# Filler matmuls in the opening of a convolution and gated feed-forward kernel: whole-array ones partly replaced by row halves and quarters

## The chip, the cores and the metric

The kernel runs on one core of one Trainium2 chip. The time is the device time of one execution in microseconds; the time before is 711.99 us, the median of three runs (711.8 to 712.13). The engines are named as in the profile: PE (TensorE matmuls) and PEld (its weight loads), DVE (VectorE), ACT (ScalarE), POOL (GpSimd) and SP (SyncE, which here only issues DMAs). PE multiplies a stationary operand (lhsT, loaded first) with a moving operand (rhs) and writes to PSUM.

## The reference

A causal convolution with a softmax over its seven taps, one tap set per head, and then a feed-forward layer whose activation is h * cos(h):

```python
w = softmax(weight)                        # 8 heads x 7 taps
x_pad = concat([zeros(6 rows), x], axis=1) # x: 8 x 4096 x 192
out[b, s, head, :] = sum_k w[head, k] * x_pad[b, s + k, head, :]   # 24 columns per head
h = out.reshape(32768, 192) @ w_in         # 192 x 2048
y = (h * cos(h)) @ w_out                   # 2048 x 192
```

Tensors come and go as float32; the kernel multiplies in bfloat16 and accumulates in float32.

## The kernel before

Tokens are handled in units of 1024 (32 units) and, for the feed-forward part, in tiles of 512 (64 tiles, t). The convolution of a unit is a matmul with a banded matrix `band` (128 x 256 per head, built from the softmax taps); its result is copied to `ct` in bfloat16, transposed to `cT` and used as the moving operand of the first feed-forward matmul.

For each tile t and each of eight j, `mm1` (L411) makes an h tile of 128 x 2 x 512: three pairs of matmuls, the two of a pair on rows 0 to 63 and 64 to 127 of the array, into the two PSUM banks of the tile. `gcu` takes the sine with a shift (ACT, L419) and multiplies it with h (DVE, L423) to give g. `mm2_step` (L458) multiplies g with w_out, again in pairs on the two row halves, 64 x 192 each, and accumulates in two banks `o_ps`. The h tiles come from a pool of three buffers, the h ring (`h_pool`); convolution results of later units use the ring as well. A new h tile can be written when the DVE product, or the copies, that read the old one are done.

The order of the work on PE and on ACT is written out by hand, in strings: `PE_FIRST[0]` for the first tile is "h0a h0b W0 h1 h2 h3 r h4 w5 d11 w4 h5 d21 W1 c11 X0 m1 h6 m11 h7 ...", where h is an mm1 (a and b its halves), m a number of mm2 steps, r, d and c convolution parts, w zero matmuls, W the cast of half of w_out, X the transpose through DMA. There is no reordering: each engine takes its queue in this order and waits where an operand or a buffer is not ready.

The opening, before that order starts, does the following. SP issues the load of the first half of unit 0 (`x_f`). DVE fills `zero`, 128 x 512 in bfloat16, with zeros. `keep_warm(n)` (L109) issues n matmuls of `zero` with `zero`, 128 x 128 stationary and 512 columns moving, into the bank `idle`; nobody reads the result. There are three of these, then the matmul that spreads the weights over the partitions (L123), then nine more. Meanwhile POOL, ACT and DVE make the softmax, a mask, `prod` and `diag` (L316, L319), and from `diag` the `band` in 16 small casts (L330, shared by DVE, POOL and ACT). ACT casts the first x to `x_bf` (L184).

`conv_first` (L347) is the next work in PE's queue after the nine: two halves of 16 matmuls with 48 columns, the first copied to `ct` by ACT, the second by DVE (L353). An SP instruction waits for the second copy and is followed on SP by four loads of w_out (`wo_f`, L97). `turn_first` (L368) transposes on PE and ACT and DVE copy the result to `cT` (L371); its four PSUM tiles are three from the h ring and one o bank. Then comes h0a, the first L411. POOL casts the x_f loads that follow (L184) and, behind them in its queue, the two halves of w_out (L93).

Of the kernel before, what the change touches and what calls it, by code (L numbers as in the profile page):

```python
# [8 lines left out]
FP32 = mybir.dt.float32  # L9
# [7 lines left out]
def kernel(  # L17
# [8 lines left out]
    nc = tc.nc  # L26
    B, S, D = x.shape
# [4 lines left out]
    T = 512  # L32
# [22 lines left out]
    h_pool = ctx.enter_context(tc.tile_pool(name="h_ps", bufs=3, space=PSUM))  # L55
# [47 lines left out]
    zero = consts.tile([128, T], BF16)  # L103
# [3 lines left out]
    def keep_warm(n, bank=idle):  # L107
        for _ in range(n):
            nc.tensor.matmul(out=bank, lhsT=zero[:, 0:128], rhs=zero, start=True, stop=True)  # L109
# [11 lines left out]
    w_all = o_pools[1].tile([128, T], FP32, name="o_ps1")  # L121
    w_bc = w_all[:, 0 : HQ * K].rearrange("p (h k) -> p h k", k=K)
    nc.tensor.matmul(out=w_all[:, 0 : HQ * K], lhsT=quarter, rhs=w_row, start=True, stop=True)  # L123
    keep_warm(9)


    xb0 = xbf_pool.tile([128, UB + 1, D], BF16, name="x_bf")
# [200 lines left out]
    for i, k in enumerate("DPDPDPDPDPDPDPAA"):  # L328
        q, rows = divmod(i, 4)
# [185 lines left out]
    for t in range(NT + 1):  # L515
# [6 lines left out]
        act, h = act.split(), {}  # L522
# [99 lines left out]
```

## Time and profile before

| | us |
|---|---|
| median of three runs | 711.99 (711.8 to 712.13) |
| the profiled execution, its own time | 711.61 |
| its span, first to last instruction | 709.9 |
| PE busy / DVE / ACT / POOL | 703.0 / 637.5 / 599.8 / 304.2 |
| first matmul | 1.31 |
| conv_first's first and last group start | 6.82, 7.90 |
| first L411 (h0a) | 10.62 |
| h7 of the first tile | 21.42 |

The page is of one profiled execution. Its times are relative to the first instruction of the program. "Busy" of PE counts the modelled length of each matmul, and matmuls overlap, so the distance from one start to the next tells the rate, and not the duration. A row of the timeline merges neighbouring instructions of one line: "x9" with a length of 3.13 are nine matmuls from the first start to the last end. A number in brackets is the idle time of that engine before the row, and the arrow names what ended it.

### The profile page before, as it was taken

The page shows a single profiled execution, that of the slowest core. Times are in us where ns is not written, and L with a number is a line of the kernel's source. Part 1 is how long each engine was busy: PE and PEld are TensorE (multiplying, and loading weights), DVE is VectorE, ACT ScalarE, POOL GpSimd, SP SyncE. Part 2 cuts the span into 40 slices and gives each one's busy share as a digit, 9 for nine tenths or more (in the row PEclk, how much of TensorE's full clock was granted, in tenths as well). Part 3 has the DMA queues.
Part 4 walks back from the last instruction along what each step waited for, and adds up shares of the span by engine and source line. Part 5 has one row for each costly group of instructions (what it writes and reads, how often), then busy time and mean ns, then how long its engine had stood idle before and what let it go on. Part 6 is the DMA issues. An engine that isn't in the chain of part 4 may idle for free.

```text
span 709.9 us, 26545 instructions
## 1 busy us (share of the span) xinstructions
PE 703.0 (99%) x11836; PEld 537.6 (76%) x11838; DVE 637.5 (90%) x598; ACT 599.8 (84%) x719; POOL 304.2 (43%) x308
## 2 busy tenths in 40 slices
PE   8999999999999999999999999999999999999997
PEld 4677777777777777777777777777777777777776
DVE  6889998998998999899999989989989999999996
ACT  7888888888888888888888888888888888888875
POOL 6653355333454433553434554335544335532400
PEclk9999999999999999999999999999999999999999
DMA  8954535535445455355354365553454554543411
GB/s 210 252 137 96 116 106 146 126 93 147 100 120 147 101 120 140 94 134 142 80 145 117 104 146 119 103 145 101 122 146 91 129 125 104 139 96 75 96 46 46
DMA packets 183713, 85.25 MB, mean 120 GB/s; under 512 B 111664, under 2 KB 183216, under 8 KB 183600
## 3 DMA queue, kind: packets, MB, share of 16 engines
q1 hardware_dynamic: 182888, 82.59, 47.9%
q8 instruction: 92, 1.51, 0.9%
q0 software_dynamic: 416, 0.79, 0.7%
q10 hardware_dynamic: 296, 0.20, 0.1%
q14 instruction: 21, 0.17, 0.1%
HBM read 31.36 MB, written 25.17 MB: 80 GB/s over the span
## 4 chain that ended last, share of the span: by engine, by line
PE 96%; DMA 1%; DVE 1%; POOL 0%; ACT 0%; SPq 0%; issue 0%; POOLq 0%
PE o_ps L458 47%; PE h L411 46%; PE h L196 3%; DMA x_f<-in_x_dram 1%; DVE g L423 0%; ACT cs L419 0%; PE h L458 0%; SPq L75 0%; POOL x_bf L184 0%; POOL mask L132 0%; PE o_ps L109 0%; ACT mask L137 0%; DVE diag L319 0%; DVE prod L316 0%; DVE o_sb L486 0%
## 5 line engine op out<-in xcount | busy, mean ns | idle before, releaser
L423 DVE TENSOR_TENSOR g<-h,cs 128x1024 bf16<-128x1024 f32 (+1 forms) x513 | 599.9, 1217 | 19.9 <-ACT cs L419 17.1
L419 ACT ACTIVATE cs<-h 128x1024 bf16<-128x1024 f32 (+1 forms) x513 | 514.4, 1022 | 85.1 <-PE h L411 64.9
L458 PEld LDWEIGHTS <-g 64*128 64x128 bf16 x8192 | 368.9, 94 | 91.6 <-DVE g L423 0.4
L458 PE MATMUL o_ps<-wo,g 64*128 64x192 bf16 x8128 | 434.8, 243 | 0.0
L411 PE MATMUL h<-cT,w 64*128 64x512 bf16 (+1 forms) x3078 | 412.2, 376 | 0.6 <-DVE g L423 0.3
L411 PEld LDWEIGHTS <-w 64*128 64x128 bf16 x3078 | 160.3, 94 | 67.4 <-issue 1.6
L302 POOL TENSOR_TENSOR edge_prod<-cT,tap 128x1008 f32<-128x1008 bf16 x30 | 67.2, 2241 | 281.7 <-DMA cT<-ct 281.7
L184 POOL CAST x_bf<-x_f 128x1728 bf16<-128x1728 f32 (+2 forms) x33 | 80.8, 2448 | 60.5 <-DMA x_f<-in_x_dram 42.3
L476 DVE COPY o_sb<-o_ps 128x384 f32<-128x384 f32 x62 | 34.6, 558 | 42.8 <-PE o_ps L458 42.6
L211 ACT CAST ct<-h 128x384 bf16<-128x384 f32 (+1 forms) x124 | 53.8, 484 | 14.0 <-PE h L196 13.4
L264 POOL COPY ct<-ct 128x1536 bf16<-128x1536 bf16 (+1 forms) x31 | 45.6, 1470 | 14.1 <-ACT ct L211 11.5
L196 PE MATMUL h<-x_bf,band 64*128 64x192 bf16 (+2 forms) x480 | 42.1, 243 | 0.1
L307 POOL TENSOR_TENSOR edge_prod<-edge_prod 128x144 f32<-128x144 f32 x60 | 33.3, 555 | 4.7
L305 POOL TENSOR_TENSOR edge_prod<-edge_prod 128x432 f32<-128x432 f32 x30 | 30.3, 1010 | 2.4
L476 ACT COPY o_sb<-o_ps 128x384 f32<-128x384 f32 x64 | 30.2, 474 | 0.1
L196 PEld LDWEIGHTS <-band 64*128 64x128 bf16 (+1 forms) x480 | 22.8, 94 | 1.5 <-issue 1.3
L308 POOL TENSOR_TENSOR cT<-edge_prod 128x144 bf16<-128x144 f32 x30 | 18.3, 610 | 2.4
L266 POOL COPY ct<-x_bf 128x192 bf16<-128x192 bf16 x60 | 19.2, 350 | 0.0
L109 PE MATMUL o_ps<-zero 128*128 128x512 bf16 x20 | 6.8, 476 | 1.4 <-DVE zero L104 1.3
L109 PEld LDWEIGHTS <-zero 128*128 128x128 bf16 x24 | 2.3, 110 | 4.2 <-issue 2.1
L93 POOL CAST wo<-wo_f 128x1536 bf16<-128x1536 f32 x2 | 2.9, 1469 | 2.4 <-DMA wo_f<-in_moe_w_out_dram 2.4
L458 PE MATMUL h<-wo,g 64*128 64x192 bf16 x64 | 3.2, 244 | 0.1
(61 smaller groups left out, 35.5 us busy)
## 6 DMA issues: line engine op xcount, KB each, us to landing
out_dram<-o_sb SPq DMA_DIRECT2D x63, 384.0 KB
x_f<-in_x_dram SPq DMA_DIRECT2D x30, 768.0 KB
x_f<-in_x_dram SPq DMA_DIRECT2D x31, 96.0 KB
x_f<-in_x_dram SPq DMA_DIRECT2D x4, 384.0 KB
wo_f<-in_moe_w_out_dram SPq DMA_DIRECT2D x4, 384.0 KB
w<-in_moe_w_in_dram POOLq DMA_DIRECT2D x2, 384.0 KB, 6.2
cT<-ct SPq DMA_TRANSPOSE x32
out_dram<-o_sb ACTq DMA_DIRECT2D x2, 96.0 KB
```

Of the source, the lines that this page charges most:

```text
L184: copy(out=bf[u][:, n0 + o : n1 + o, :].rearrange("p n (h k r) -> p (n h) k r", k=NC, r=R), in_=x_tiles[u][:, n0:n1, :].rearrange("p n (h ...
L196: return nc.tensor.matmul(out=ps[i // 2][:, 0 : (n1 - n0) * 2 * G].rearrange("p (n k i r) -> p i n k r", n=n1 - n0, k=NC, i=2)[:, i % 2], ...
L211: copy(o[:, :, 0, :], i[:, :, 0, :])
L264: nc.gpsimd.tensor_copy(out=ct[:, 0:nb, :, 1, :], in_=ct[:, 0:nb, :, 0, :])
L302: nc.gpsimd.tensor_tensor(out=edge_prod, in0=window, in1=tap.rearrange("p (a b k) -> p a b k", a=1, b=1).to_broadcast([128, NC * UB, K - 1 ...
L305: nc.gpsimd.tensor_tensor(out=edge_prod[:, :, :, 0:3], in0=edge_prod[:, :, :, 0:3], in1=edge_prod[:, :, :, 3:6], op=ALU.add)
L307: nc.gpsimd.tensor_tensor(out=edge_prod[:, :, :, 0], in0=edge_prod[:, :, :, 0], in1=edge_prod[:, :, :, j], op=ALU.add)
L411: nc.tensor.matmul(out=h[:, i, n0 * 128 : n1 * 128], lhsT=w[rows, k, j, :], rhs=c[rows, m0 + n0 : m0 + n1, k, :], start=(k == 0), stop=(k ...
L419: nc.scalar.activation(out=cs[:, :, part], in_=h[:, :, part], func=AF.Sin, bias=math.pi / 2.0, scale=1.0)
L423: nc.vector.tensor_tensor(out=g_tiles[t][:, 2 * j : 2 * j + 2, part], in0=h[:, :, part], in1=cs[:, :, part], op=ALU.mult)
L458: ms.append(nc.tensor.matmul(out=o_ps[tt, b, si], lhsT=g_tiles[tt][rows, f, s * 128 : (s + 1) * 128], rhs=wo[rows, f // 2, f % 2, :], star ...
L476: (copy or copies[b])(o_sb[t][:, 2 * b : 2 * b + 2, :].rearrange("p s d -> p (s d)"), o_ps.pop((t, b)))
```

## The change

After L123, of the nine zero matmuls five stay. Then a tile is taken from the h ring, and a string of 19 letters is gone through, each of which issues matmuls on parts of `zero` into that tile:

- p: two matmuls on the row halves (64 rows, 128 columns of the array), 512 columns moving, one into each bank;
- o: the same with 192 columns moving;
- q: four matmuls on the quarters of the array (64 rows by 64 columns), 192 columns moving; the two column halves of a row half write to partitions 0 to 63 and 64 to 127 of its bank.

There are 6 p, 4 o and 9 q, 56 matmuls in all. Nobody reads the tile.

```diff
-    keep_warm(9)
+    keep_warm(5)
+    tiles = h_pool.tile([128, 2, T], FP32, name="h")
+
+    def warm_tiles(kinds):
+
+        for k in kinds:
+            for r in range(2):
+                for c in range(2) if k == "q" else range(1):
+                    rows = slice(64 * r, 64 * r + 64)
+                    m = slice(64 * c, 64 * c + 64) if k == "q" else slice(0, 128)
+                    nc.tensor.matmul(out=tiles[m, r, 0 : T if k == "p" else D], lhsT=zero[rows, m],
+                                     rhs=zero[rows, 0 : T if k == "p" else D], start=True, stop=True,
+                                     skip_group_check=True)
+
+    warm_tiles("ppqppqqoqooqqqqopqp")
```

The result of the kernel does not depend on these matmuls. No other line is changed; the lines below move down by 14.

## The prediction

> **What bounds the kernel now.** I read the page first: who is busy, and the chain that ended last.
>
> ```profile
> span 709.9 us, 26545 instructions
> PE 703.0 (99%) x11836; PEld 537.6 (76%) x11838; DVE 637.5 (90%) x598; ACT 599.8 (84%) x719; POOL 304.2 (43%) x308
> PE 96%; DMA 1%; DVE 1%; POOL 0%; ACT 0%; SPq 0%; issue 0%; POOLq 0%
> ```
>
> PE is the bound nearly everywhere. To see where it is not, I asked for the busy time in stretches (columns: stretch, its length, PE, PEld, DVE, ACT, POOL with instruction counts, clock, DMA share, GB/s).
>
> ```profile
> 6.40:10.60 4.20, 2.93 (x46) 1.93 (x48) 3.02 (x9) 2.44 (x6) 1.47 (x6) 1.00 0.98 185
> 10.60:21.40 10.80, 10.17 (x104) 5.38 (x106) 7.66 (x8) 9.81 (x15) 6.89 (x8) 1.00 1.15 280
> 21.40:706.30 684.90, 684.74 (x11672) 528.51 (x11671) 622.56 (x569) 582.49 (x693) 291.09 (x280) 1.00 0.48 117
> ```
>
> From 21.4 us on PE is busy 684.74 of 684.90 us. So the time is "when does the dense part begin" plus a fixed 685 us and a tail, and the change can act only through the opening. That I read in order of time (start, duration, engine, line; in brackets the idle time before and its releaser).
>
> ```profile
> 3.23 3.13 PE L109 MATMUL o_ps<-zero 128*128 128x512 bf16 x9
> ...
> 4.49 0.15 PEld L109 LDWEIGHTS <-zero 128*128 128x128 bf16 x1 [0.28 <-issue]
> ...
> 4.91 0.15 PEld L109 LDWEIGHTS <-zero 128*128 128x128 bf16 x1 [0.28 <-issue]
> ...
> 5.33 0.53 PEld L109 LDWEIGHTS <-zero 128*128 128x128 bf16 x3 [0.27 <-issue]
> ...
> 6.82 0.26 PE L347 MATMUL o_ps<-x_bf,band 128*128 128x48 bf16 x4 [0.46 <-ACT x_bf L184]
> ...
> 7.90 0.98 PE L347 MATMUL o_ps<-x_bf,band 128*128 128x48 bf16 x24 [0.32 <-DVE band L330]
> 8.52 0.80 ACT L353 CAST ct<-o_ps 128x768 bf16<-128x768 f32 x1 [1.21 <-PE o_ps L347]
> ...
> 8.92 0.96 DVE L353 CAST ct<-o_ps 128x768 bf16<-128x768 f32 x1 [1.02 <-PE o_ps L347]
> ...
> 10.62 1.62 PE L411 MATMUL h<-cT,w 64*128 64x256 bf16 x18 [0.18 <-DVE cT L371]
> ```
>
> The nine zero matmuls follow at 0.42 to 0.43 us as far as the one at 4.91, and at 0.216 us from 5.33 on: TensorE ran at half speed until about 5.3 us in this execution (the page's clock figure does not show it). The last of the nine starts at 5.98, so PE is free from 6.20. Its first useful work of this stage, conv_first (L347), then waits for x_bf and band until 6.82 and, in steps, until 7.90. So these nine cost nothing: they lie in a gap.
>
> How much cover is behind that gap I read from the h ring:
>
> ```profile
> 11.16 3.26 ACT L419 ACTIVATE cs<-h 128x512 bf16<-128x512 f32 x4 [0.37 <-PE h L411]
> ...
> 16.95 2.36 DVE L423 TENSOR_TENSOR g<-h,cs 128x1024 bf16<-128x1024 f32 x2 [1.26 <-ACT cs L419]
> ...
> 21.42 0.82 PE L411 MATMUL h<-cT,w 64*128 64x512 bf16 x6
> ```
>
> ACT is busy 9.81 of the 10.80 us from 10.6 to 21.4. It starts with the first h tile (11.16) and goes without a pause of 0.1 us through the Sins and conv copies as far as 18.67. DVE's third-tile product (16.95) waits for that ACT queue, and its end at 18.18 releases the ring slot of h5, which starts at 18.23. The chain on the page takes another way there: x_f landing 15.21, POOL cast to 16.83, conv of unit 1 at 16.87, the four zero matmuls of "w4" to 18.1. The two ways meet within 0.1 us. After h5 its Sin and product follow, and h7 (21.42) waits for that product, which ends at 21.37. So a later first h tile makes h5, and with it 21.42, later by the same amount: there is no slack behind conv_first.
>
> **The change part by part.** *Removed:* four 512-column zero matmuls. The fifth of the nine starts at 4.91, the next would start at 5.33, so the new stream begins at 5.33.
>
> *Added:* 6 "p" (pairs of row halves, 512 columns), 4 "o" (pairs of row halves, 192 columns) and 9 "q" (four quarters, 192 columns): 12 + 8 + 36 = 56 matmuls. All are in the same PE queue ahead of conv_first.
> - p: L411's pairs of 64x512 run side by side: x6 from 25.01 to 25.66, 0.216 a pair. 6 x 0.216 = 1.30.
> - o: L458's pairs of 64x192: x26 from 23.94 to 25.01, 0.0825 a pair. 4 x 0.0825 = 0.33.
> - q: no row of this trace splits the array's columns. Low end: all four together, no faster than matmuls can start on one array; L347's first four start within 0.26 - 0.18 = 0.08 us, 0.025 each, so 0.10. High end: one after another, 4 x 0.0825 = 0.33. Between: the row halves side by side as in L458, the two column halves in turn, 0.165. I take 0.165, being the nearest row plus what no row shows to overlap: 9 x 0.165 = 1.49.
> - Changes of the array's split: a stretch of 16 x 0.0425 of L379 starting at 13.94 should end at 14.62, and L411 (halves) starts at 14.73; six L411 from 14.73 should end at 15.38, L109 starts at 15.48. 0.11 each. The string has 10 changes between halves and quarters, plus one in and one out: 12 x 0.11 = 1.32. Low end: a change from halves to quarters costs nothing, leaving 0.22. High end: each waits for the pipeline to empty, 0.243 duration less 0.0825 spacing = 0.16: 1.92.
>
> Sum 1.30 + 0.33 + 1.49 + 1.32 = 4.44; conv_first can start at 5.33 + 4.44 = 9.77. By then band and x_bf are there, so its 32 matmuls go at 0.025: the ACT copy of half 0 starts 15 x 0.025 + 0.18 + 0.03 = 0.59 after, the DVE copy 0.99 after. Against 8.52 and 8.92 that is 1.84 late. From there copies, transposes (L368) and copies follow in the same chain. h0a started 0.13 after its releaser (DVE, 10.49) where h0b took 0.04 (11.05 to 11.09), and the second w load landed at 10.54: 0.09 of slack. Delay of the dense part: 1.75 us.
>
> *Moved behind it:* SP waits for the DVE copy of half 1 before the four wo loads (issued from 9.90), so these go out 1.84 later. The x_f loads ahead of them do not wait for PE, and DMA is full until about 18 us, so I expect wo to land nearly as before (17.44; its cast ends 19.03 and is needed at 19.46, which moves too). The transpose at 16.02 and the loads behind it on SP wait for ACT copies and move with the rest. POOL's casts of x_f stay where they are.
>
> *The tile:* one more "h" buffer of three, written by PE alone; nobody waits for it, and the ring is only turned by one. 0, unless the planner then hands out a slot that is still held; the cover is PE's own order.
>
> [...]
>
> The profiled execution took 711.61 with a span of 709.9 (1.7 around it); the three runs have a median of 711.99, 0.38 more. The delay is added to each: 713.4 for a profile, **713.7** for the median.
>
> **The rivals.** The bound between same and changed is 0.2%, 1.42 us, about what a measurement of this kernel can tell from no change.
> 1. *Quarters run four at a time* (0.10): sum 3.85, 1.16 late, 713.15. For it: halves do so. Against: no row. It counts as "same".
> 2. *Quarters in single file* (0.33): sum 5.92, 3.24 late, 715.2. The pairs' side-by-side rows speak against it, but the shape is new.
> 3. *Dear changes or a late clock.* At 0.16 a change: 714.3. The half-speed stretch ended at 5.33 here, 4.0 us after PE's first matmul; in another execution it may end 1 to 2 us later, and the new stream, now on the path, would take 0.5 to 1 longer: 714.2 to 714.7. Before, the gap hid that. [...]
> 4. *Everything fits in the gap:* quarters 0.10 and free changes among halves and quarters: sum 2.75, conv_first at 8.08, 0.06 late: 712.05, not slower. It decides below a sum of about 4.1.
> 5. *Faster:* PE works only 2.93 of 4.20 us between 6.4 and 10.6. If the clock falls back there in the timed runs, filling the gap saves it. But the timed runs lie only 0.38 above a profile whose L368 and L411 rows are at full speed: at most 711.6 to 711.7. A gain of 1.42 has no place in the opening.
> That the stream is not made at all can be left out: PE takes its queue in order.
>
> **How the numbers follow.** My sum (quarters in two turns, changes 0.11, each term off by a little) 0.45, of which 0.38 over the bound; case 1 0.16; case 2 0.14; case 3 0.12; case 4 0.08; case 5 0.05. Slower 0.38 + 0.14 + 0.12 = 0.64; same 0.07 + 0.16 + 0.08 = 0.31; faster 0.05. Range: leaving out cases 4 and 5 (0.13) and the far end of 2 and 3 together (0.06), from 712.6 (case 1 with the ten inner changes at half price, 1.16 - 10 x 0.055 = 0.61 late) to 715.4 (case 2). My sum alone, a quarter either way: 713.2 to 714.2.
>
> **What would show it.** Right: after the fifth full matmul, rows of p at 0.216; quarters in groups of 0.165; 0.11 of pause at each change; conv_first in one run from about 9.8 with no wait for band; first L411 near 12.4; h7 near 23.2; the dense stretch as long as before, 684.9. Quarters starting together, or no pauses, show case 1 or 4. Zero matmuls at 0.43 beyond 5.33 show the late clock. The prediction is wrong at its root if h5 or the dense part starts at the old time although conv_first is late, or if the dense part changes its length.

## The result and the profile after

The changed kernel takes 713.57 us (median of 18 runs, 712.48 to 713.89); the kernel before takes 711.67 us in 18 runs beside it (711.59 to 712.13). The ratio is 1.0022, 95% interval 1.0015 to 1.0029: slower by 1.90 us. The forecast was 713.7 in a range of 712.6 to 715.4. The number is nearly exact, but several of its terms were off, in opposite directions, as the traces below show.

The page of the changed kernel, whose profiled execution took 712.78 us:

```profile
span 711.1 us, 26651 instructions
PE 705.2 (99%) x11890; PEld 536.0 (75%) x11890; DVE 637.3 (90%) x598; ACT 599.9 (84%) x719; POOL 304.4 (43%) x308
PE 98%; ACT 1%; DVE 1%; issue 0%
```

The DMA that held 1% of the chain before is gone from it: the chain now reaches back through the opening's PE, ACT and DVE work. Its stretches (columns as before):

```profile
9.00:11.80 2.80, 2.57 (x49) 1.68 (x48) 1.66 (x3) 1.59 (x3) 0.00 (x0) 1.00 1.07 309
11.80:22.60 10.80, 10.09 (x105) 5.43 (x106) 7.64 (x8) 9.81 (x15) 7.60 (x8) 1.00 1.11 271
22.60:707.50 684.90, 684.76 (x11672) 526.12 (x11671) 622.43 (x569) 582.53 (x693) 290.55 (x279) 1.00 0.48 117
```

The last two stretches are cut at the lengths of before, from the new h0a and the new h7; their content is that of before (ACT busy 9.81 us in the one, PE 684.76 with the same 11672 matmuls in the other). That the lengths themselves are kept, the starts of h0a and h7 and the end of the last matmul show: from h7 (22.61) to that end (707.61) are 685.00 us, and before (21.42 to 706.43) 685.01. Everything lies before h0a. The timeline of the opening:

```profile
3.23 2.30 PE L109 MATMUL o_ps<-zero 128*128 128x512 bf16 x5
...
5.46 3.69 PE L134 MATMUL h<-zero 64*128 64x512 bf16 x56
...
9.09 0.97 PE L361 MATMUL o_ps<-x_bf,band 128*128 128x48 bf16 x32
9.70 0.80 ACT L367 CAST ct<-o_ps 128x768 bf16<-128x768 f32 x1 [2.41 <-PE o_ps L361]
...
11.80 1.62 PE L425 MATMUL h<-cT,w 64*128 64x256 bf16 x18 [0.18 <-DVE cT L385]
...
19.41 0.82 PE L425 MATMUL h<-cT,w 64*128 64x512 bf16 x6 [0.26 <-DVE g L437]
...
22.61 0.82 PE L425 MATMUL h<-cT,w 64*128 64x512 bf16 x6 [0.15 <-DVE g L437]
```

The 56 part matmuls run from 5.46, and conv_first (now L361) starts at 9.09 and goes through in one run: its operands were ready, so only PE's queue held it. ACT waited 2.41 us for it where it had waited 1.21. h0a went from 10.62 to 11.80, h5 from 18.23 to 19.41, h7 from 21.42 to 22.61: 1.18, 1.18 and 1.19 later. What is lost ahead of conv_first arrives whole at the dense part.

Starts of the matmuls in one piece of the stream, as the trace has them (us):

```
q  6.741 6.744 6.748 6.751     after a p that started at 6.432
q  6.848 6.851 6.854 6.858
o  7.033 7.036
q  7.218 7.222 7.225 7.228
...
q  7.803 7.807 7.810 7.813     second to fourth of four in a row:
q  7.886 7.889 7.893 7.896     0.0825 from one to the next
q  7.968 7.972 7.975 7.978
```

Four quarters start within 0.010 us of each other and take 0.0825 together, as long as one pair of halves. From the p at 6.432 to the next q are 0.309, 0.093 more than the 0.216 that a p takes; the first spacing after a change is longer too (0.107 instead of 0.0825 for a q, 0.227 instead of 0.216 for a p). As a whole: from 5.33 to conv_first at 9.09 are 3.76 us; 6 p, 4 o and 9 q by these spacings are 1.30 + 0.33 + 0.74 = 2.37, and 1.39 is left for the twelve changes, 0.12 each.

This one profile explains 1.17 us (712.78 against 711.61), the medians differ by 1.90. Where the rest is, the first experiment shows.

### The profile page after: what moved, and what is told of

It is laid out like the page before. It is cut to its first block, busy times and chain, and to the rows that moved or that the text cites. A ratio compares the mean times of both kernels' runs of the same rounds, so it can differ in the third digit from the quotient of the medians.

```text
span 711.1 us, 26651 instructions
## 1 busy us (share of the span) xinstructions
PE 705.2 (99%) x11890; PEld 536.0 (75%) x11890; DVE 637.3 (90%) x598; ACT 599.9 (84%) x719; POOL 304.4 (43%) x308
## 4 chain that ended last, share of the span: by engine, by line
PE 98%; ACT 1%; DVE 1%; issue 0%
PE o_ps L472 47%; PE h L425 46%; PE h L210 3%; DVE g L437 1%; PE o_ps L109 1%; ACT cs L433 1%; PE h L134 1%; PE h L472 0%; ACT ct L400 0%; ACT ct L367 0%; DVE cT L385 0%; PE o_ps L123 0%; PE h L382 0%; PE o_ps L361 0%; PE o_ps L393 0%
## 5 line engine op out<-in xcount | busy, mean ns | idle before, releaser
L425 PEld LDWEIGHTS <-w 64*128 64x128 bf16 x3078 | 158.7, 94 | 68.6 <-issue 1.9
L134 PE MATMUL h<-zero 64*64 64x192 bf16 (+2 forms) x56 | 3.7, 282 | 0.0
```

Of the source, the lines that this page charges most:

```text
L425: nc.tensor.matmul(out=h[:, i, n0 * 128 : n1 * 128], lhsT=w[rows, k, j, :], rhs=c[rows, m0 + n0 : m0 + n1, k, :], start=(k == 0), stop=(k ...
```

## The experiments

**The changed kernel again.** No line differs from the changed kernel; only the executions do.

> The changed kernel once more, as the yardstick on this chip. Theory L (the length of the zero stream stands on PE's path to conv_first, and grows when TensorE's clock rises late): about 1.9 us over before in the median, single executions from 0.8 to 2.2 over, and the profile's conv_first start, less 7.93, gives its own excess. Rival D (the spread comes from loads landing at different times): the excess does not follow conv_first's start.

> The changed kernel, one look. Theory W (the spread of its times is the moment at which TensorE's clock rises, and half of any delay of it is paid before conv_first): with the rise at u, conv_first starts at about 9.09 + 0.45 (u - 5.38), as 5.38 gave 9.09 and 6.06 gave 9.37, and the end of the last matmul follows 698.5 us after conv_first's start. An execution of about 713.6 should show a rise between 6.5 and 8. Rival D (loads): the last matmul's end moves without conv_first's start.

> The same kernel and the same two expectations as the other look: another moment of the rise, the same line.

> The changed kernel, one look more, for an execution in the upper part of its times (713.3 to 713.9). Theory W: the line of the looks before (rise 5.04, 5.38, 5.98, 6.06 with conv_first at 8.92, 9.09, 9.33, 9.37): 9.09 + 0.42 (u - 5.38); at 713.6 the rise lies near 7.2 and conv_first starts near 9.9. Rival D: an execution of that time with conv_first below 9.5.

> As the other look: the same line, another moment of the rise.

The further timing of the changed kernel gave a median of 713.25 us in 11 runs (712.52 to 713.76) against 711.65 for the kernel before: 1.0020 (1.0011 to 1.0029). The six traces of it, ordered by the moment at which the trace's record of TensorE's granted clock goes from half to full speed (us):

| execution | clock rises | conv_first starts | last matmul ends | time |
|---|---|---|---|---|
| look2 | 5.04 | 8.92 | 707.43 | 712.62 |
| the profile after | 5.38 | 9.09 | 707.61 | 712.78 |
| look3 | 5.98 | 9.33 | 707.85 | 713.03 |
| again | 6.06 | 9.37 | 707.90 | 713.08 |
| look5 | 7.46 | 9.96 | 708.48 | 713.69 |
| look4 | 7.89 | 10.12 | 708.64 | 713.81 |

Two ends of the table in their timelines, first look2, then look4:

```profile
3.23 2.13 PE L109 MATMUL o_ps<-zero 128*128 128x512 bf16 x5
5.29 3.69 PE L134 MATMUL h<-zero 64*128 64x512 bf16 x56
8.92 0.97 PE L361 MATMUL o_ps<-x_bf,band 128*128 128x48 bf16 x32
```

```profile
3.23 2.31 PE L109 MATMUL o_ps<-zero 128*128 128x512 bf16 x5
5.48 4.71 PE L134 MATMUL h<-zero 64*128 64x512 bf16 x56
10.12 0.97 PE L361 MATMUL o_ps<-x_bf,band 128*128 128x48 bf16 x32
```

The same 56 matmuls take 3.69 us in one execution and 4.71 in the other, because in the second the clock rises 2.85 us later; (10.12 - 8.92) / 2.85 = 0.42 us of delay for each microsecond. The last matmul ends 698.51 to 698.53 us after conv_first's start in all six. So the spread of 1.4 us among the runs of the changed kernel is the moment of the rise and nothing else that these traces show: the rival that loads make it has no support here. In the runs of before, most lie within 0.1 us: there the gap hides the moment of the rise, as `halves4` below shows at a rise of 7.06.

**The same stream with fewer changes of the split.**

```diff
-    warm_tiles("ppqppqqoqooqqqqopqp")
+    warm_tiles("ppppppooooqqqqqqqqq")
```

> The same 56 part matmuls, but all p first, then all o, then all q: three changes of the array's split in place of twelve. Theory L with a price of 0.09 to 0.11 per change: the stream is 0.8 to 1.0 us shorter, conv_first at 8.1 to 8.3 with an early clock, and 0.8 to 1.0 below the changed kernel. Rival Q (the quarters cost, not the changes): less than 0.3 us below the changed kernel.

Measured: 712.25 us in 11 runs (711.69 to 713.01), ratio to before 1.0008 (0.9999 to 1.0016), 1.00 below the changed kernel timed with it. The profile taken had a late rise, 7.77:

```profile
5.48 3.78 PE L134 MATMUL h<-zero 64*128 64x512 bf16 x56
9.19 0.97 PE L361 MATMUL o_ps<-x_bf,band 128*128 128x48 bf16 x32
```

By the table's line the changed kernel would start conv_first at 9.09 + 0.42 x (7.77 - 5.38) = 10.09 with that rise, so nine changes fewer are worth 0.90 us there, 0.10 each (0.11 by the medians). The rival that the quarters themselves cost falls.

**Whole matmuls in place of the parts,** once into the bank `idle` (full22), once into an h tile (full22h); both against the changed kernel:

```diff
 # full22
-    keep_warm(5)
-    tiles = h_pool.tile([128, 2, T], FP32, name="h")
...
-    warm_tiles("ppqppqqoqooqqqqopqp")
+    keep_warm(22)
```

```diff
 # full22h
     keep_warm(5)
     tiles = h_pool.tile([128, 2, T], FP32, name="h")
...
-    warm_tiles("ppqppqqoqooqqqqopqp")
+    keep_warm(17, tiles[:, 0, :])
```

> 22 whole zero matmuls in place of five and the string of parts: 17 x 0.216 = 3.67 us from 5.33, so conv_first at about 9.0 with an early clock, the changed kernel's 9.09. Theory L: the same excess over before as the changed kernel within 0.2 us in the median (1.7 to 2.1). Rival K (the halves and quarters cost something of their own, by their changes of the split that outlast the stream, or by raising the clock later than whole matmuls do): 0.5 us or more below the changed kernel.

full22 took 713.59 us in 10 runs (712.76 to 714.68), 1.0027 (1.0017 to 1.0036), and so 0.34 above the changed kernel, where 0.2 were expected at most and the rival wanted it below. The two intervals overlap, so the medians alone do not settle the 0.34, but its trace (rise at 7.17) has a pause of about that size:

```profile
3.24 6.85 PE L109 MATMUL o_ps<-zero 128*128 128x512 bf16 x22
10.23 1.04 PE L347 MATMUL o_ps<-x_bf,band 128*128 128x48 bf16 x32
```

The last zero matmul ends at 10.09 and starts at 9.70. conv_first follows 0.53 after that start instead of the 0.216 that a matmul of 512 columns takes, and four by four with small pauses. The waits name the zero matmul as releaser: conv_first takes a new tile in the bank which the last zero matmul had just written. In the kernel before this wait ends in the gap, and in the changed kernel the bank's last zero matmul ends 3.6 us earlier.

> 22 whole zero matmuls again, the last 17 into a tile of the h ring instead of the bank that conv_first writes. Theory P (conv_first waited 0.31 us after 22 whole ones because the last of them wrote its bank): it now starts 0.22 to 0.25 us after the start of the last zero matmul, in place of 0.53. Rival X (the pause belongs to whole matmuls followed by band's weight loads): 0.5 us again.

```profile
5.34 4.61 PE L109 MATMUL h<-zero 128*128 128x512 bf16 x17
9.78 0.96 PE L349 MATMUL o_ps<-x_bf,band 128*128 128x48 bf16 x32
```

The last zero matmul starts at 9.57, conv_first 0.216 later: with another bank, and nothing else changed, the pause is gone. With the rise at 6.90, this execution (713.52) starts conv_first at 9.78; the changed kernel's line gives 9.73. Whole matmuls of the same total length cost what the parts cost; in this one execution the kind of matmul makes no difference.

**Only the removal.** Against the kernel before:

```diff
-    keep_warm(9)
+    keep_warm(5)
```

> Only the removal: five whole zero matmuls and nothing after them; PE then idles from about 5.4 until x_bf and band are there at 6.82. Theory L: within 0.3 us of before, since the four removed ones lay in the gap. Rival C (the fill is needed to raise or hold the clock): 0.5 to 1.5 us slower than before, with conv_first or the transposes at half speed in the profile.

Measured: 713.05 us in 11 runs (712.43 to 713.27), 1.0018 (1.0009 to 1.0026). Nine of the runs lie between 713.00 and 713.27 and two at 712.4; one of the nine was traced. Here my theory falls and the rival holds. In its timeline conv_first, the fillers of turn_first, the transposes and the first h tiles are slow:

```profile
6.80 0.32 PE L347 MATMUL o_ps<-x_bf,band 128*128 128x48 bf16 x4 [1.25 <-ACT x_bf L184]
...
7.88 1.28 PE L347 MATMUL o_ps<-x_bf,band 128*128 128x48 bf16 x24 [0.24 <-DVE band L330]
...
8.99 1.03 PE L109 MATMUL h<-zero 128*128 128x512 bf16 x2
...
9.81 0.85 PE L368 MATMUL h<-ident,ct 128*128 128x128 bf16 x6
...
11.65 2.21 PE L411 MATMUL h<-cT,w 64*128 64x256 bf16 x18
```

conv_first starts on time (6.80), but its 24 last matmuls take 1.28 instead of 0.98, the six transposes 0.85 instead of 0.51, the first eighteen L411 2.21 instead of 1.62. The clock rises at 13.12 in this execution. The four removed matmuls lay in a gap, and yet they are worth 1.4 us: with them, in the profile before, the clock rises at 5.31, ahead of the work that counts; without them, in this execution, it rises behind most of the opening.

**A short fill of parts,** as long as the four removed ones; against the changed kernel:

```diff
-    warm_tiles("ppqppqqoqooqqqqopqp")
+    warm_tiles("pppp")          # halves4; quarters10: warm_tiles("qqqqqqqqqq")
```

> Five whole zero matmuls and four p: as much PE time as the nine whole ones of before, PE free at about 6.4 with an early clock, conv_first at 6.82 again. Theory B (pairs of halves hold PE as busy as whole ones for the clock): within 0.3 us of before in the median. Rival N (halves do not count in full): the clock rises late as with five alone, 0.8 to 1.6 us over before.

> Five whole zero matmuls and ten q, again free at about 6.4. Theory B: within 0.3 us of before. Rival N (quarters with 192 columns do not count in full): 0.8 to 1.6 us over before, with the rise of the clock near 13 us as with five alone.

halves4 took 711.66 us in 11 runs (711.60 to 712.00), 1.0001 (0.9992 to 1.0010); quarters10 took 711.82 (711.58 to 712.37), 1.0002 (0.9993 to 1.0011); before stood at 711.64. Both within 0.2 us of before: pairs of halves and groups of quarters do here what the whole matmuls did. The last 24 matmuls of conv_first take 0.98 us in both traced executions, as in the profile before, against 1.28 in `five`. halves4's profiled execution had a rise as late as 7.06:

```profile
5.48 1.80 PE L134 MATMUL h<-zero 64*128 64x512 bf16 x8
7.21 0.37 PE L361 MATMUL o_ps<-x_bf,band 128*128 128x48 bf16 x8
7.88 0.98 PE L361 MATMUL o_ps<-x_bf,band 128*128 128x48 bf16 x24 [0.29 <-DVE band L344]
...
9.34 0.51 PE L382 MATMUL h<-ident,ct 128*128 128x128 bf16 x6
...
10.59 1.62 PE L425 MATMUL h<-cT,w 64*128 64x256 bf16 x18 [0.18 <-DVE cT L385]
```

At half speed the short fill stretches itself to 7.2, which is still inside the gap: the last 24 matmuls wait for band at 7.88, as before, the rows behind them have full speed, and the time is 711.63. The profile of quarters10 shows one more source of spread. In that execution (712.16) the first half of h0a is held by the second load of w:

```profile
10.61 0.27 PE L425 MATMUL h<-cT,w 64*128 64x256 bf16 x1 [0.18 <-DVE cT L385]
11.15 1.47 PE L425 MATMUL h<-cT,w 64*128 64x256 bf16 x17 [0.27 <-DMA w<-in_moe_w_in_dram]
```

That load landed at 11.10 instead of 10.54, and cost about half a microsecond. In the traces of the changed kernel it could not show: h0a starts at 11.63 or later there.

None of these kernels is faster than the one before; its 32 runs beside the first set of experiments lie between 711.58 and 712.48, and halves4 reaches the same times and no better ones. No version that beats both came into sight.

## Why the prediction was right

*The bound and the path.* Right. The dense part kept its length, 685.00 us from h7 to the last matmul against 685.01, the stretch from h0a to h7 its 10.80, and a delay of conv_first reaches the end unshortened: the difference between the end of the last matmul and the start of the last matmul of conv_first is 697.7 us in the profile before (8.70 to 706.43), in the profile after (9.88 to 707.61), in full22 (11.09 to 708.82) and in sorted (9.98 to 707.71). The 0.09 us of slack that the sum took off at the second load of w is not there: h0a starts 0.15 after the end of the copy that releases it in both profiles (10.47 to 10.62, 11.66 to 11.80), and it came 1.18 later, as the copy of half 0 did.

*Removed: the new stream begins at 5.33, and the four cost nothing.* Right for this change, because the added stream keeps PE busy in their place, but the reading "these nine cost nothing" was incomplete: in the run with the removal alone the four that went were worth 1.4 us. The predicted sum did not use that, so it did no harm.

*Added: p and o.* As priced. Two o in a row start 0.0825 apart in sorted. Every second p in the trace after stands behind a change and starts 0.227 after the first; the 0.01 more is counted with the changes.

*Added: q.* Mis-sized. The sum took 0.165, two turns of 0.0825; the four quarters run together in 0.0825, the first after a change in 0.107. The trace before had no row for a split of columns, and I let "no row shows it" weigh against all four together. The trace after shows them together, with four starts within 0.010 us. This term was 0.7 us too large (9 x 0.08).

*Changes of the split, 12 x 0.11.* Right in kind and nearly in size: 0.12 each by what the stream leaves in the trace after (0.093 of pause and the longer first spacing), 0.10 to 0.11 by the sorted string; all twelve are 0.07 more than the 1.32 of the sum. The alternatives of free changes (case 4) and of 0.16 per change are out.

*The sum.* For an execution with the rise where the profile before had it, conv_first was forecast at 9.77 and came at 9.09; case 1 had 9.18. So by the mechanism of an early clock it was the first rival that came true: 1.16 forecast, 1.17 measured between the two profiles. Even that agreement joins two errors of 0.09: the stream was that much shorter, and the slack was missing.

*The late clock.* This was part of case 3, with a chance of 0.12 for the whole case, and it is the common case. The traces of the changed kernel have rises from 5.04 to 7.89, worth up to 1.2 us, and a median of 713.57 corresponds to a rise near 7.2 by the line of the table. I had one trace, took its moment of the rise for the usual one, and let the forecast stand on it. The price named in case 3, half a microsecond for each microsecond of delay, was right in kind: 0.42. The later rise adds about 0.75 to the median, which happens to cancel the 0.7 that the quarters were overpriced. In the terms of the sum: 1.75 - 0.74 (q) + 0.07 (changes) + 0.09 (slack) = 1.17, which is the difference of the two profiles, and the other 0.73 of the measured 1.90 is the late rise. That the forecast lies so near the result is therefore luck; its side and its range are not, as both cases were inside.

*The base.* The median before was 711.67 in the later runs and 711.99 in the three that I had, so the excess is 1.90 and not the 1.75 of the sum, although the time itself is 0.1 below the forecast.

*Moved behind it.* Not quite as expected, and without effect. In the trace after, POOL's first cast of w_out starts at 18.41 instead of 17.57, and its third cast of x_f, which was to stay where it is, at 16.12 instead of 15.33. Over the six traces of the changed kernel the latter start varies from 15.06 to 16.14, and the last matmul still ends 698.5 us after conv_first's start in each.

*Faster.* The case that filling the gap gains something found nothing: the runs of before lie 0.1 us from their fastest, in the median.

*What stays open:* what decides the moment of the rise in an execution. It was observed in all the traces and not steered. What the traces show is how busy PE was ahead of it. In the 3.413 us up to the rise (the last section has this length) PE is busy throughout in twelve of the thirteen traces, where the rise lies between 5.04 and 7.89, and in 94% of them in that of `five` (9.70 to 13.12); in the 3.413 us before those, it is busy at most 93% (look4, 1.06 to 4.47). Whether this decides the moment no run tests, and why the moment differs between executions of one program was not shown.

## What to carry to other kernels

Filler matmuls have a window: they should last until TensorE's clock has risen, also in the executions where it rises late (here 5.04 to 7.89), and end before the operands of the first useful matmul are ready (here the band for the last 24 matmuls of conv_first, 7.90). What lasts longer was paid in full here, where PE bounds the rest: between the two profiles conv_first's second copy starts 1.18 later (8.92 to 10.10), and the last matmul ends 1.18 later (706.43 to 707.61). A filler that lies in a gap is not free to remove (1.4 us in `five`, with the rise at 13.12): ask what the clock does without it. When one profile shows a clock rise, price the opening for other moments of it too, since in these traces what stands on the path takes about twice as long per column until then (a zero matmul of 512 columns 0.43 us instead of 0.216).

## What the runs showed of the hardware

- The moment of the clock's rise varies from execution to execution of one program: between 5.04 and 7.89 us after the first instruction in the six of the changed kernel, with PE busy from 1.3 us on. The start of the stretch at full speed moves by 2.85 us between executions of one program; its length takes three values in the traces of all kernels, 699.73, 703.15 and 706.56 us (703.146 in the profile before, 706.559 in the profile after). They lie 3.41 to 3.42 apart and are 205, 206 and 207 times 3.413.
- With five matmuls after the first three and L123, PE busy from 1.31 to 5.54 us, the clock had not risen when conv_first started at 6.80 in the traced execution of `five`; it rose at 13.12. With four p behind the five (halves4), PE busy from 1.31 to 7.28, it rose at 7.06. In look4, PE busy from 1.31 on, it rose at 7.89. Each is one execution.
- Four quarter matmuls of 64 x 64 with 192 columns take 0.0825 us together, as a pair of halves does; a change of the split at full speed is a pause of 0.09 to 0.11 us beyond the usual spacing, between halves and quarters (p at 6.432 to q at 6.741) as between halves and whole (the last p at 8.765, conv_first at 9.087).
- A matmul into a new tile in a bank that PE itself wrote last started 0.53 us after the start of the last 512-column matmul (full22, 9.70 to 10.23), and 0.216 when the bank was another (full22h, 9.57 to 9.78).
